# Retention and expert layers on one core: two more units fetched in pieces, and routing's constants two half units later

## The chip, the cores and the metric

The kernel runs on one core of a Trainium2 chip. The metric is the device time in microseconds (us) of one execution. The engines of the core work side by side, each through its own instructions in a fixed order: TensorE (PE; PEld is its weight load), VectorE (DVE), ScalarE (ACT), GpSimd (POOL) and SyncE (SP, which here only issues transfers). They wait for each other and for transfers through semaphores.

## The reference

Two layers follow each other.

```python
scores = scale * np.matmul(q, k.transpose(0, 1, 3, 2))      # 8 batches, 8 heads, 576 positions, 64 wide
gamma = 1.0 - 2.0 ** (-5.0 - np.arange(H))
Dmat = np.where(rel >= 0, gamma ** rel, 0.0)                # rel = query position - key position
x = np.matmul(scores * Dmat, v)                             # then 4608 tokens x 512
logits = x @ w_gate                                         # 8 experts, 576 tokens each at most
# all (token, expert) logits from the largest down: a token goes to the first expert that has room
out[mask] = np.maximum(x[mask] @ w1[e], 0.0) @ w2[e]        # 512 -> 1024 -> 512, expert by expert
```

## The kernel before

The first layer (`attention`, the first 125 us or so) is cut into 16 units, each two batches by two heads; a unit takes two half units, g = 0 and g = 1, so half unit 2u+g runs from 0 to 31. A unit needs four arrays: `q` and `k` (128 x 1152, transposed), `v` (128 x 1152) and `n` (128 x 1024, keys in rows). Decay is split into blocks of 128 positions: within a block a masked product, between blocks a running state.

What each engine does for unit u, in the order in which it does it:

- POOL: `qscale` multiplies `q` by decays in place, in three instructions (columns 0 to 512, 512 to 1024, 1024 to 1152; L619); then `kscale` makes `ks` from `n` in two instructions (L624). For units 2 and up all five are emitted together at the end of unit u-2 (L878 to L880), so POOL meets them in just this order: three of `q`, then two of `ks`.
- PE: `scores` (L634, L639), `update` (L655: state += ks' v; `pS`), `from_states` (L669) and `from_blocks` (L678, L684) into `px`. In half unit 2u+1 PE runs `scores` of unit u+1's first half, and then `update(u+1, 0)`, the first user of that unit's `ks` and `v`.
- DVE: `masks` (L644 `at`, L646 `am`) multiplies the scores by the decay mask. ACT copies the state out (`st`, L658) and the output (`xT`, L693).

Every engine takes its instructions in the order in which the code emits them; nothing is rearranged. Work that has its place between the units hangs in a table: `at(i, f)` puts f at the end of half unit i, and `fills` runs what stands there. Routing's preparation hangs there: `setup` (twelve steps of DVE memsets and ACT copies that read the constants `rc_f`), `share` (four DVE copies, L169 to L172, that put small constants into the PSUM tile `PT`, columns 288 to 475) and, from half unit 8 on, `logits` (PE, L710, writes columns from 0 of the same tile `PT`) and `logits2` (DVE reads them).

Transfers: units 0 and 1 come in pieces (columns up to 512, then the rest), the others whole. SP issues them from one queue. Each transfer has one of eight semaphores in turn, and SP waits before it issues one until the transfer that last had that semaphore has landed: eight are under way at most. `ahead(u)` and the loop around it (L816, L851, L863) issue what comes next; the tiles of four units (three of `n`) fit.

After the first layer come a search that fills the experts in turn and, per expert, a gather, two matrix products (L1110, L1153) and a scatter. Weights are fetched once the search has named the expert. Nothing there is touched.

Of the kernel before, what the change touches and what calls it, by code (L numbers as in the profile page):

```python
# [558 lines left out]
def attention(tc, nc, P, qk, vk, cst_d, wg_d, rf, xd, Lg, raw):  # L559
# [17 lines left out]
    def load(u, what, cuts=None):  # L577

        bp, hp = divmod(u, HP)
        for i in what:  # L580
            n = 1024 if i == "n" else 1152
            t = P['ld'].tile([128, n], F32, name=i + "in", bufs=3 if i == "n" else 4)
            src = qk[bp, hp, "qk".index(i)] if i in "qk" else vk[bp, hp, :, :1152] if i == "v" else vk[bp, hp, :, 1152:]
            LD[u, i] = t
            if cuts:
                pieces[u, i] = [(t[:, a:b], src[:, a:b]) for a, b in zip((0,) + cuts, cuts + (n,))]
            else:
                nc.sync.dma_start(t, src)

    pieces = {}  # L590
# [14 lines left out]
    R = Route(P['c'], P['a'], P['ps'], Lg, P['ident'])  # L605
# [4 lines left out]
    PT = P['ps'].tile([128, 512], F32, name="pT", tag="t")  # L610
# [166 lines left out]
    def at(g, f, *a):  # L777
        fill.setdefault(g, []).append((f, a))
# [8 lines left out]
        at(2*hp - 2, decays, hp)  # L787
    setup = R.setup()
    for i in range(12):
        at(4 + i, lambda: next(setup, None))  # L790
    at(6, lambda: R.share(PT[:, 288:475]))
    for bp in range(NP - 1):
        for i, x in enumerate(((0, 4), (4, 9))):
            at(8*(bp+1)+2*i, logits, bp, *x)
# [20 lines left out]

    def ahead(u):  # L816
        if u == 0:
            load(2, "qknv")
            load(3, "qkn")
            R.fetch(nc, rf)  # L820
        if u + 3 < 16:
            load(u + 3, "v")
        if u == 1:
            for b in range(2):
                for h in range(2):
                    nc.sync.dma_start(wg[64*h:64*h+64, :, b, 0:8], wg_d.rearrange("(hp h p) e -> h p hp e", h=2, p=64)[h ^ b])
# [18 lines left out]
    last = 15  # L845
    for u in range(16):
        ahead(u)
        for g in range(2):
            n, m = (u, u + 1)[g], (1, 0)[g]
# [375 lines left out]
def build(tc, nc, qk, vk, cst, wg, rf, w1, w1n, w2, out):  # L1225
    with ExitStack() as top:
# [23 lines left out]
        with ExitStack() as ctx:  # L1250
            P['wt'] = "px"
            P['pp'] = ctx.enter_context(tc.tile_pool(name="a_ps", bufs=1, space=bass.MemoryType.PSUM))
            Q = dict(P)
            for name, bufs in (("a", 1), ("ld", 2), ("w", 2), ("xt", 2)):
                Q[name] = ctx.enter_context(tc.tile_pool(name="a_" + name, bufs=bufs))
            R, rows = attention(tc, nc, Q, qk, vk, cst, wg, rf, xd, Lg, P['raw'])

            def idle(what):

                if what in ("row", "rows"):  # L1260
                    for i in range(2):
                        if rows:
                            if i or what == "rows" or len(rows) < 14:
                                rows.pop(0)()
                        elif i or what == "rows":
                            warm(1 + (what == "rows"))
                    what = 0
                if what:
                    warm(what)
            R.idle = idle  # L1270
            run = moe(tc, nc, P, R, xd, (w1, w1n), w2, out, mix)
            mix.drain(lambda: 0 in run.regs)
            while rows:
                rows.pop(0)()
# [22 lines left out]
```

## Time and profile before

| | us |
|---|---|
| median of 3 runs | 610.39 (610.30 to 612.76) |
| profiled execution | 610.37 |
| its span (first to last instruction) | 608.6 |
| PE busy | 593.4 |
| POOL busy | 245.8 |

The profile is of one execution. Its span leaves 1.77 us around it. "PE busy 98%" counts overlapping matmuls as busy and is no measure of peak; what matters below is where PE has nothing to do, and for whom it then waits.

### The profile page before, as it was taken

The numbers are of one execution on the slowest core, as the hardware profiler recorded it, in microseconds if no ns is written. First come the engines' busy times: TensorE is split into PE (matmuls) and PEld (weight loads), VectorE is DVE, ScalarE is ACT, GpSimd is POOL, SyncE is SP. The second block draws the span as 40 slices with busy tenths as digits, with TensorE's granted clock in tenths as the row PEclk, the third lists the DMA queues.
The fourth block names the chain that finished last, engine by engine and source line by source line (L and its number), as shares of the span: only waits on it lengthen the run. The fifth ranks groups of instructions, "written<-read, shape, count | busy, mean of one in ns | idle before, by whom it ended". The sixth has DMA issues, their size and how long they took to land.

```text
span 608.6 us, 14908 instructions
## 1 busy us (share of the span) xinstructions
PE 593.4 (98%) x5778; PEld 515.2 (85%) x5778; DVE 421.6 (69%) x1510; ACT 254.3 (42%) x446; POOL 245.8 (40%) x313
## 2 busy tenths in 40 slices
PE   8899999999999999999999999999999999999994
PEld 5788888875798889879977997898899889989983
DVE  5647687787899878878866885788488845544400
ACT  2344333334563654434561554266244334423310
POOL 5778456613411641441431243133224758610021
PEclk9999999999999999999999999999999999999998
DMA  9999999766786798794985699288938734420010
GB/s 324 407 367 403 306 358 378 254 198 205 190 224 149 224 263 162 259 246 124 263 231 153 135 251 248 85 195 242 249 90 193 229 119 146 150 78 27 2 44 34
DMA packets 49450, 124.84 MB, mean 205 GB/s; under 512 B 7011, under 2 KB 19811, under 8 KB 49379
## 3 DMA queue, kind: packets, MB, share of 16 engines
q1 hardware_dynamic: 36130, 80.10, 37.5%
q0 software_dynamic: 13104, 43.53, 31.5%
q8 instruction: 45, 0.74, 0.5%
q10 hardware_dynamic: 144, 0.26, 0.1%
q14 instruction: 27, 0.21, 0.1%
HBM read 80.35 MB, written 18.87 MB: 163 GB/s over the span
## 4 chain that ended last, share of the span: by engine, by line
PE 77%; issue 12%; DMA 5%; POOL 3%; DVE 2%; SPq 0%; ACT 0%; POOLq 0%; DVEq 0%
PE ph L1110 29%; PE py L1153 26%; PE sc L634 5%; PE px L678 4%; PE pS L655 3%; DMA vin<-in_vk 3%; PE px L669 3%; PE pt L1074 2%; PE r L383 2%; PE pT L710 2%; POOL out_y L1130 1%; POOL xg L1030 1%; PE r L489 1%; DMA kin<-in_qk 1%; DMA raw<-in_w 1%
## 5 line engine op out<-in xcount | busy, mean ns | idle before, releaser
L1153 PE MATMUL py<-w2h,hb 128*128 128x512 f32 x576 | 187.3, 397 | 0.0
L1110 PE MATMUL ph<-xh,w1h 128*128 128x320 f32 (+1 forms) x512 | 151.9, 301 | 0.2 <-ACT xh L1076 0.2
L1110 PE MATMUL ph<-xl,w1h 128*128 128x320 f32 (+1 forms) x512 | 149.2, 296 | 0.0
L1110 PE MATMUL ph<-xh,w1l 128*128 128x320 f32 (+1 forms) x512 | 149.0, 296 | 0.0
L1153 PE MATMUL py<-w2l,hb 128*128 128x512 f32 (+1 forms) x320 | 125.1, 391 | 0.0
L1153 PEld LDWEIGHTS py<-w2h,hb 128*128 128x128 f32 x576 | 104.5, 188 | 21.7
L1110 PEld LDWEIGHTS ph<-xh,w1h 128*128 128x128 f32 x512 | 96.0, 189 | 1.3 <-ACT xh L1076 0.7
L1114 ACT ACTIVATE hb<-ph 128x256 fp32r<-128x256 f32 (+1 forms) x128 | 52.4, 409 | 106.0 <-PE ph L1110 104.2
L1110 PEld LDWEIGHTS ph<-xl,w1h 128*128 128x128 f32 x512 | 96.2, 190 | 0.3
L1110 PEld LDWEIGHTS ph<-xh,w1l 128*128 128x128 f32 x512 | 96.0, 189 | 0.0
L1130 POOL DMA_INDIRECT out_y<-yt,idx x40 | 40.2, 1004 | 129.3 <-ACT yt L1173 67.0
L1119 DVE SCALAR_TENSOR_TENSOR hb<-ph,hb 128x256 fp32r<-128x256 f32 (+1 forms) x192 | 57.8, 350 | 26.1 <-ACT hb L1114 25.4
L1153 PEld LDWEIGHTS py<-w2l,hb 128*128 128x128 f32 (+1 forms) x320 | 56.7, 177 | 13.0
L619 POOL TENSOR_TENSOR qin<-qin,cst 128x512 f32<-128x512 f32 (+1 forms) x48 | 47.7, 1020 | 35.5 <-DMA qin<-in_qk 31.5
L1173 ACT ACTIVATE yt<-py 128x512 f32<-128x512 f32 x31 | 18.5, 598 | 92.3 <-PE py L1153 66.3
L658 ACT ACTIVATE st<-pS,cst 128x128 f32<-128x128 f32 x64 | 23.6, 368 | 75.0 <-PE pS L655 75.0
L1009 POOL DMA_DIRECT2D w2l<-raw x24 | 21.7, 905 | 73.3 <-ACT w2l L1008 36.8
L646 DVE TENSOR_TENSOR am<-sc,cst 128x1024 f32<-128x1024 f32 x32 | 39.0, 1218 | 15.9 <-PE sc L634 15.9
L1042 POOL DMA_INDIRECT xg<-xd,idx x30 | 30.4, 1015 | 42.7 <-DVE room L524 16.1
L1030 POOL DMA_INDIRECT xg<-xd,quarter x36 | 36.9, 1026 | 10.8 <-issue 8.1
L1009 POOL DMA_DIRECT2D w1l<-raw x23 | 21.1, 933 | 41.9 <-ACT w1l L1008 33.6
L634 PE MATMUL sc<-qin,kin 64*128 64x128 f32 x512 | 37.5, 286 | 0.2 <-DMA kin<-in_qk 0.2
(213 smaller groups left out, 931.8 us busy)
## 6 DMA issues: line engine op xcount, KB each, us to landing
raw<-in_w SPq DMA_DIRECT2D x56, 512.0 KB, 5.8
w2l<-raw POOLq DMA_DIRECT2D x24, 512.0 KB, 6.8
w1l<-raw POOLq DMA_DIRECT2D x23, 512.0 KB, 6.9
qin<-in_qk SPq DMA_DIRECT2D x14, 576.0 KB, 7.6
kin<-in_qk SPq DMA_DIRECT2D x14, 576.0 KB, 8.8
vin<-in_vk SPq DMA_DIRECT2D x14, 576.0 KB, 9.9
nin<-in_vk SPq DMA_DIRECT2D x14, 512.0 KB, 8.6
xd<-raw SPq DMA_DIRECT2D x36, 128.0 KB, 5.2
```

Source lines behind the costliest of these rows:

```text
L619: nc.gpsimd.tensor_tensor(x, x, e[:, None, :n].to_broadcast([128, (b-a)//n, n]), op=ALU.mult)
L634: nc.tensor.matmul(t[:, h, 128*j:128*j+128], blk(k, 4*g+j)[r], blk(q, 4*g+j)[r], start=(j == 0), stop=True, skip_group_check=True)
L646: nc.vector.tensor_tensor(a, SC[u, g].rearrange("p h (j q) -> p h j q", q=128), m1[:, u % HP, :, None, :].to_broadcast([128, 2, 4, 128]), ...
L678: nc.tensor.matmul(PX[u, g][y:y+64, b, 128*c:128*c+128], blk(v, 4*g+j)[:, 64*h:64*h+64], AM[u, g][:, h, j], start=False, stop=True, skip_g ...
L1009: add = lambda: nc.gpsimd.dma_start(lo, raw, accum_op=ALU.add)
L1030: nc.gpsimd.indirect_dma_start(out=t[:, k, :], out_offset=None, in_=xq[:, :], in_offset=bass.IndirectOffsetOnAxis(ap=quarters[e][:, v:v+1] ...
L1042: nc.gpsimd.indirect_dma_start(out=xg[:n, j, :], out_offset=None, in_=xd[:, :], in_offset=bass.IndirectOffsetOnAxis(ap=found[e][:n, j:j+1] ...
L1110: T.matmul(ps, w, x, start=(k == 0), stop=(k == 11))
L1114: A.activation(hb[:, f, c], ps, AF.Relu)
L1119: V.scalar_tensor_tensor(hb[:, f, to+a:to+b], ps[:, a:b], 0.0, hb[:, f, 256*s+a:256*s+b].bitcast(F32), op0=ALU.max, op1=ALU.subtract)
L1130: st = nc.gpsimd.indirect_dma_start(out=out[:, :], out_offset=bass.IndirectOffsetOnAxis(ap=found[e][:n, t:t+1], axis=0), in_=y[:n], in_off ...
L1153: T.matmul(ps[:m], a, w, start=(k == 0), stop=(k == last), skip_group_check=True)
```

## The change

```diff
     setup = R.setup()
     for i in range(12):
-        at(4 + i, lambda: next(setup, None))
-    at(6, lambda: R.share(PT[:, 288:475]))
+        at(6 + i, lambda: next(setup, None))
+    at(8, lambda: R.share(PT[:, 288:475]))
...
     def ahead(u):
         if u == 0:
-            load(2, "qknv")
-            load(3, "qkn")
+            for x in (2, 3):
+                load(x, "kqnv", (512,))
+                for _ in range(2):
+                    for i in "kqnv":
+                        nc.sync.dma_start(*pieces[x, i].pop(0))
             R.fetch(nc, rf)
-        if u + 3 < 16:
+        elif u + 3 < 16:
             load(u + 3, "v")
```

Units 2 and 3 now come as units 0 and 1 do: the first 512 columns of k, q, n and v, then the rest of k, q, n and v. The constants `rc_f` (610 columns, 305 KB) follow all of unit 3, where they stood ahead of its `v`. All twelve steps of `setup`, and `share`, run two half units later.

On SP, whose rows are transfers, in the place after the second piece of unit 1's `v`: eight rows of before,

```order
L588 DMA qin<-in_qk 128x1152 [waits DMAHW2_49]
L588 DMA kin<-in_qk 128x1152 [waits DMAHW3_49]
L588 DMA nin<-in_vk 128x1024 [waits DMAHW4_49]
L588 DMA vin<-in_vk 128x1152 [waits DMAHW5_49]
L588 DMA qin<-in_qk 128x1152 [waits DMAHW6_49]
L588 DMA kin<-in_qk 128x1152 [waits DMAHW7_49]
L588 DMA nin<-in_vk 128x1024 [waits DMAHW0_49,Pool_49]
L101 DMA rc_f<-in_rf 128x610 [waits DMAHW1_49]
```

and the eight of the change, which are unit 2 alone:

```order
L822 DMA kin<-in_qk 128x512 [waits DMAHW2_49]
L822 DMA qin<-in_qk 128x512 [waits DMAHW3_49]
L822 DMA nin<-in_vk 128x512 [waits DMAHW4_49]
L822 DMA vin<-in_vk 128x512 [waits DMAHW5_49]
L822 DMA kin<-in_qk 128x640 [waits DMAHW6_49]
L822 DMA qin<-in_qk 128x640 [waits DMAHW7_49]
L822 DMA nin<-in_vk 128x512 [waits DMAHW0_49]
L822 DMA vin<-in_vk 128x640 [waits DMAHW1_49]
```

The whole `q` stood first; now its second piece is the sixth transfer of its unit.

On POOL, unit 2's five instructions (`qin` is `q`, `ks` the scaled keys; "waits DMAHW7" is a wait for a transfer), before:

```order
L619 TENSOR_TENSOR qin<-qin,cst 128x512 [waits DMAHW2_49]
L619 TENSOR_TENSOR qin<-qin,cst 128x512
L619 TENSOR_TENSOR qin<-qin,cst 128x128
L624 TENSOR_TENSOR ks<-nin,cst 128x512 [waits DMAHW4_49,PE_49,Pool_49]
L624 TENSOR_TENSOR ks<-nin,cst 128x512
```

and of the change:

```order
L619 TENSOR_TENSOR qin<-qin,cst 128x512 [waits DMAHW3_49]
L619 TENSOR_TENSOR qin<-qin,cst 128x512 [waits DMAHW7_49]
L619 TENSOR_TENSOR qin<-qin,cst 128x128
L624 TENSOR_TENSOR ks<-nin,cst 128x512 [waits DMAHW4_49,PE_49,Pool_49]
L624 TENSOR_TENSOR ks<-nin,cst 128x512 [waits DMAHW0_49]
```

The order is the same; the second instruction has a wait of its own, for the second piece of `q`, and both `ks` stand behind it.

On PE, at the end of half unit 8, where the first `logits` stand (`pT` is the tile `PT`), before:

```order
L655 MATMUL pS<-vin,ks 64x64 [waits Activation_49]
L655 MATMUL pS<-vin,ks 64x64 x3
L710 MATMUL pT<-xT,wg 32x128 [waits DMAHW7_49,DMAHW0_49]
L710 MATMUL pT<-xT,wg 32x128
L710 MATMUL pT<-xT,wg 32x128 [waits DMAHW2_49,DMAHW1_49]
L710 MATMUL pT<-xT,wg 32x128 x13
```

and of the change:

```order
L655 MATMUL pS<-vin,ks 64x64 [waits Activation_49]
L655 MATMUL pS<-vin,ks 64x64 x3
L710 MATMUL pT<-xT,wg 32x128 [waits DMAHW7_49,DMAHW0_49,DVE_49]
L710 MATMUL pT<-xT,wg 32x128
L710 MATMUL pT<-xT,wg 32x128 [waits DMAHW2_49,DMAHW1_49]
L710 MATMUL pT<-xT,wg 32x128 x13
```

The first of them waits for DVE now. On DVE `share`, which writes `pT` too, stands in half unit 8 directly behind that half unit's `am`:

```order
L644 TENSOR_TENSOR at<-px,cst 128x256 [waits PE_49]
L646 TENSOR_TENSOR am<-sc,cst 128x1024
L169 COPY pT<-rc_f 128x128
L170 COPY pT<-rc_f 128x8 [waits DVE_49]
L171 COPY pT<-sm 128x10 [waits DVE_49]
L172 COPY pT<-inc 128x5 [waits DVE_49]
```

In the program the semaphore count for which the first `logits` wait is that of the fourth of these copies, L172.

## Rows read from the trace of the kernel before

**Rows 1.** The page, chain that ended last: shares of the span by engine.

```profile
PE 77%; issue 12%; DMA 5%; POOL 3%; DVE 2%; SPq 0%; ACT 0%; POOLq 0%; DVEq 0%
```

**Rows 2.** Chain that ended last, in order of time: start us, us, what.

```profile
7.26 5.79 DMA vin<-in_vk
...
13.07 10.12 DMA vin<-in_vk
```

**Rows 3.** Timeline of PE: start us, us, instruction, count [idle before <-releaser].

```profile
19.46 0.94 PE L669 MATMUL px<-qin,st 64*64 64x128 f32 x24
20.63 1.16 PE L634 MATMUL sc<-qin,kin 64*128 64x128 f32 x16 [0.22 <-DMA kin<-in_qk]
23.32 0.45 PE L655 MATMUL pS<-vin,ks 128*64 128x64 f32 x8 [1.53 <-DMA vin<-in_vk]
...
30.19 0.45 PE L655 MATMUL pS<-vin,ks 128*64 128x64 f32 x8
```

**Rows 4.** Waits of PE from 23 to 125 us: total us, times, longest.

```profile
PE pS L655 <- DMA vin<-in_vk: 1.5, 1, 1.5
```

**Rows 5.** Timeline of SP's queue: issues of unit 1.

```profile
5.60 0.43 SPq L602 DMA_DIRECT2D kin<-in_qk  x1
...
10.38 0.33 SPq L602 DMA_DIRECT2D vin<-in_vk  x1
```

**Rows 6.** Transfers issued from 9.8 to 10.6 us: count, KB, us to landing.

```profile
vin<-in_vk SPq DMA_DIRECT2D x1, 320.0 KB, 7.3
```

**Rows 7.** Transfers issued from 5.5 to 6.4 us.

```profile
kin<-in_qk SPq DMA_DIRECT2D x1, 256.0 KB, 5.4
```

**Rows 8.** Timeline of POOL.

```profile
8.24 1.69 POOL L619 TENSOR_TENSOR qin<-qin,cst 128x512 f32<-128x512 f32 x2 [0.84 <-DMA qin<-in_qk]
9.88 1.04 POOL L624 TENSOR_TENSOR ks<-nin,cst 128x512 f32<-128x512 f32 x1
...
19.13 2.91 POOL L619 TENSOR_TENSOR qin<-qin,cst 128x512 f32<-128x512 f32 x3 [1.21 <-DMA qin<-in_qk]
22.00 2.04 POOL L624 TENSOR_TENSOR ks<-nin,cst 128x512 f32<-128x512 f32 x2
...
32.60 2.92 POOL L619 TENSOR_TENSOR qin<-qin,cst 128x512 f32<-128x512 f32 x3 [2.90 <-DMA qin<-in_qk]
35.48 2.04 POOL L624 TENSOR_TENSOR ks<-nin,cst 128x512 f32<-128x512 f32 x2
```

**Rows 9.** Busy time by stretch: engines (instructions), PEclk, DMA share, GB/s.

```profile
9.00:12.00 3.00, 3.00 (x58) 2.64 (x60) 1.23 (x3) 0.74 (x2) 2.33 (x5) 1.00 1.05 396
...
21.00:24.00 3.00, 1.47 (x31) 1.31 (x30) 3.00 (x4) 0.13 (x1) 3.00 (x4) 1.00 1.01 403
```

**Rows 10.** Timeline of DVE, half units 6 and 8.

```profile
34.06 1.21 DVE L646 TENSOR_TENSOR am<-sc,cst 128x1024 f32<-128x1024 f32 x1
35.20 0.28 DVE L169 COPY pT<-rc_f 128x128 f32<-128x128 f32 x1
...
35.92 0.17 DVE L172 COPY pT<-inc 128x5 int32<-128x5 int32 x1
...
40.94 1.21 DVE L646 TENSOR_TENSOR am<-sc,cst 128x1024 f32<-128x1024 f32 x1
```

**Rows 11.** Timeline of PE, half unit 8.

```profile
41.96 1.08 PE L710 MATMUL pT<-xT,wg 128*32 128x128 f32 x32
```

**Rows 12.** Line L1248 (warm-up matmuls) to 8 us: duration ns min/median/max, first, last.

```profile
L1248 PE MATMUL warm<-full x12: 607/634/634, 1.5 to 6.1; 128*128 128x512 bf16 x12
```

**Rows 13.** The same line from 100 to 200 us.

```profile
L1248 PE MATMUL warm<-full x49: 376/379/395, 142.1 to 157.9; 128*128 128x512 bf16 x49
```

**Rows 14.** Busy time by stretch, the end (columns as in rows 9).

```profile
600.00:605.00 5.00, 0.68 (x4) 0.22 (x2) 0.41 (x1) 0.40 (x1) 0.96 (x1) 0.96 0.14 52
605.00:608.60 3.60, 0.00 (x0) 0.00 (x0) 0.00 (x0) 0.00 (x0) 0.00 (x0) 0.50 0.00 0
```

**Rows 15.** Timeline of PE, its last matmul.

```profile
600.29 0.39 PE L1153 MATMUL py<-w2l,hb 128*128 128x512 f32 x1
```

## The prediction

> **What bounds the kernel now.** I read the chain of waits first. It runs over PE for most of the span and over DMA for 5% [rows 1]; put in order of time, its DMA part lies in the first 23 us, and its last piece there is unit 2's whole `v`, issued at 13.07 and landed 10.12 later, at 23.19 [rows 2]. From there on the reader should see only PE. The timeline of PE shows what that transfer holds: `scores` of unit 2 at 20.63 after 0.22 us of waiting for `k`, and `update(2, 0)` at 23.32 after 1.53 us of waiting for `v` [rows 3]. The view of PE's waits from 23 to 125 us has that one row alone [rows 4], so from 23.32 to the end of the first layer PE has no other wait worth naming, and everything after (search, weights, experts) hangs on PE's results. A microsecond gained or lost at `update(2, 0)`, or by a wait put into PE's row later, therefore moves the end by a microsecond. At most the two waits, 0.22 + 1.53 = 1.75 us, can be gained.
>
> But `update(2, 0)` has two parents. It also wants POOL's first `ks` of unit 2. In POOL's timeline [rows 8] the three `q` instructions start at 19.13 and the two `ks` at 22.00, 1.04 us each (a lone one, 9.88, shows it): the first is ready at 23.04. It is 0.15 us earlier than `v`. So taking `v` away uncovers POOL at once.
>
> **The pieces of unit 2.** When do they land? All transfers share one queue and land in turn. The last piece of unit 1 was issued at 10.38 [rows 5] and took 7.3 [rows 6]: it landed at 17.68. From there to 23.19 the four whole transfers of unit 2, 576 + 576 + 512 + 576 = 2240 KB, took 5.51 us, 2.46 us per 1000 KB. Pieces are a little slower: unit 1's first `k` piece landed at 5.60 + 5.4 = 11.00 [rows 5, 7], its first `v` piece, three pieces of 256 KB later, at 7.26 + 5.79 = 13.05 [rows 2]: 2.05 us for 768 KB, 2.67 per 1000 KB. These are the two bounds. In the change unit 2's pieces come as k, q, n, v of 256 KB, then k and q of 320 KB: the second piece of `q` ends 1664 KB after 17.68, at 17.68 + 4.09 = 21.77 by the one, at 17.68 + 4.44 = 22.12 by the other. I take the middle, 21.95.
>
> POOL now. The first piece of `q` (512 KB after 17.68, at about 19.0) finds POOL idle, as before (its 1.21 us of idling ended at 19.13). Its first instruction ends near 20.3, and PE, whose `from_states` ends at 19.46 + 0.94 = 20.40, goes into `scores` without a wait, to 20.40 + 1.16 = 21.56. There the 0.22 is gained. But then POOL stands before the second part of `q`, whose piece lands at 21.95, and the `ks` instructions stand behind it. What is left to do from that landing to the end of the first `ks` is what unit 0 shows in the same form: two `q` instructions at 8.24, and `ks` to 9.88 + 1.04 = 10.92, 2.68 us [rows 8]. With 0.08 us from landing to start and 0.1 us from POOL to PE (`v`'s hand-over took 23.19 to 23.32), `update(2, 0)` starts at 21.95 + 0.08 + 2.68 + 0.1 = 24.81 instead of 23.32: **+1.5 us** (1.3 to 1.7 between the two rates). `v`'s first piece has long landed (1000 KB after 17.68, near 20.3) and its wait is gone; what is late next is POOL.
>
> A wait in POOL's row is passed on to what is queued behind it. The second `ks` of unit 2 ends about 1 us later, near 25.7, and `update(2, 2)` comes over 3 us after `update(2, 0)`: covered. Unit 3: its second `q` piece lands one unit (2240 KB, 5.5 to 6.0 us) after unit 2's, at 27.5 to 28.1, its first `ks` is ready 2.8 us after that, at 30.3 to 30.9. Before, `update(3, 0)` ran at 30.19 [rows 3], so 1.5 us later it runs at 31.7 and finds it there. This cover is the first delay itself. Unit 4 is whole again; its `q` started on POOL at 32.60, and the bytes ahead of it are the same, so its `ks` (35.48 + 1.04 = 36.5) comes when it did, with PE 1.5 us later.
>
> **More transfers.** Units 2 and 3 come in 16 pieces instead of 8 whole transfers. An issue takes SP 0.33 to 0.43 us [rows 5], 8 more take some 3 us of SP's time over the 15 us in which they are issued, and SP idles between issues, since it waits for one of eight semaphores each time: no cost, as the queue stays full. The stretch from 9 to 12 us, all pieces, moved 396 GB/s, that from 21 to 24 us, whole transfers, 403 [rows 9]: the price of pieces, already in the upper bound above. The landings of pieces follow each other by 0.68 us [rows 2, 5, 7]. The Trainium skill (DMA: Bandwidth & Descriptors, Anatomy of one DMA) speaks against more and smaller transfers: about 2 us fixed for each. By that, as an estimate from the page, eight more, one after another, would cost 16 us and the sum would be near 629; the landings don't bear it out here, since transfers under way together share that time, and I give it no chance.
>
> **Constants two half units later.** `rc_f` lands behind unit 3's `v`, near 30, where its first user now stands in half unit 6 (DVE was at 34.06 there): covered. The ACT copies of `setup` sit in ACT's idle time in any half unit and nobody waits for them soon: nothing. Moving DVE's memsets costs nothing either; half unit 6 loses `share` and gains them.
>
> `share` is another matter. In half unit 6 nobody on PE touched `pT` for two half units. In half unit 8 PE's first `logits` write the same tile, and they now wait for the fourth copy (shown in the order of PE's rows above). In half unit 6 `share` ended at 35.92 + 0.17 = 36.09, 2.03 us after the `am` ahead of it began, at 34.06 [rows 10]. In half unit 8 `am` began at 40.94, so `share` would end at 40.94 + 2.03 = 42.97 on the old clock. PE came to the `logits` at 41.96 [rows 11]. With 0.06 us of hand-over PE stands for 42.97 + 0.06 - 41.96 = **1.07 us**. DVE's `am` hangs on PE's matmuls, so both have shifted alike and the difference holds. Bounds: 0, were DVE done earlier, and 1.3 if the copies run a third slower beside POOL. I take 1.07: they ran beside POOL in half unit 6 too (32.60 to 37.5).
>
> **Sum.** Against the profiled execution's own 610.37 (0.02 below the median of the runs): 610.37 + 1.5 + 1.07 = **612.9 us**, +0.42%. About 0.5%, 3.05 us, is what a measurement of this kernel can tell from no change, so the forecast is a small loss inside "same", its own range 612.2 to 613.5.
>
> **Rivals.**
>
> 1. The clock falls: the side of "slower". PE stands idle from 21.56 to 24.81, 3.25 us, in one piece. The trace has waits of 1.53 us at most in this layer, and the granted clock stays 1.00 there [rows 9]. It falls once: the last matmul ends at 600.68 [rows 15], and the stretch from 600 to 605 averages 0.96, the next is 0.50 [rows 14], the 1.2 GHz level; 0.04 lacking of 5 us at half speed is 0.4 us, so the fall came near 604.6, 3.9 us after the matmul. 3.25 us lies between the wait that did nothing and the one that did. Price: at the start of the kernel the warm-up matmuls take 634 ns each [rows 12], later 379 [rows 13], and all twelve, from 1.5 to 6.7 us, are slow, so half speed lasts 5.2 us or more after work begins and loses half of that, 2.6 us: 612.9 + 2.6 = 615.5. It decides once the idle piece comes near 3.9 us. The Trainium skill (TensorE: Matmul & The Clock Gate, HAM oscillation) describes such a fall between bursts that wait for transfers. No wait in this trace is long enough to tell. Chance 0.15.
>
> 2. POOL is not held: the second `q` piece lands so early that `ks` is back at 23.0 or before, which takes a landing by 20.2. The landings above give at least 21.77, against it [rows 2, 5 to 7]. Only `share` would cost: 610.4 + 1.07 - 0.1 = 611.4. Chance 0.1.
>
> 3. The change does what it says and `share` does not hold PE: both waits go, 610.37 - 1.75 = 608.6. It needs an early `ks` and a DVE that runs ahead; neither row gives it. Chance 0.04. With only `share` not in the way it is 611.9: chance 0.06.
>
> **Numbers.** Forecast 0.65, the rivals 0.15, 0.1, 0.04 and 0.06. The range 611.2 to 614.8 holds the forecast, rival 2, the second half of rival 3 and what of rival 1 ends with a short slow spell, some 0.84. Slower by over 0.5% (above 613.4): rival 1 and a tenth of the forecast's part, 0.23. Faster by over 0.5% (below 607.3) would need more than the two waits hold: 0.03. The rest, 0.74, is same.
>
> **What would show it.** Right: POOL's second `q` instruction of unit 2 idle until about 22 with the transfer as releaser; PE's `pS` of unit 2 idle about 3.2 us until POOL's `ks`, at 24.8; PE's first L710 idle about 1.1 us until DVE's L172, and PE without other new waits to 125 us. Wrong: `pS` of unit 2 before 23.5; no wait at L710; a granted clock under 1.00 after 24 us (rival 1); or a new wait of unit 3's `update` on POOL, which would add what it shows.

## The result and the profile after

| | before | change |
|---|---|---|
| median of six runs each, us | 611.13 (610.30 to 612.76) | 615.56 (614.56 to 616.02) |
| profiled execution, us | 610.37 | 615.68 |
| its span, us | 608.6 | 613.9 |
| mean granted clock of that execution | 0.997 | 0.994 |

The ratio is 1.0065, 95% interval 1.0047 to 1.0084: slower by 0.65%, 2.7 us above the forecast of 612.9 and 0.8 above the end of its range.

The two views that show it at once are PE's waits from 23 us to the last `logits` (total us, times, longest), which answer to [rows 4]:

```profile
PE pS L655 <- POOL ks L624: 3.1, 1, 3.1
PE px L669 <- issue: 1.1, 1, 1.1
PE pT L710 <- DVE pT L172: 1.0, 1, 1.0
```

and PE's timeline around unit 2, which answers to [rows 3] (start us, us, instruction, count, idle before and its releaser):

```profile
20.50 1.16 PE L634 MATMUL sc<-qin,kin 64*128 64x128 f32 x16
24.81 0.45 PE L655 MATMUL pS<-vin,ks 128*64 128x64 f32 x8 [3.15 <-POOL ks L624]
25.09 1.15 PE L678 MATMUL px<-am,vin 128*64 128x128 f32 x16
...
27.66 1.93 PE L634 MATMUL sc<-qin,kin 64*128 64x128 f32 x16
...
33.20 0.45 PE L655 MATMUL pS<-vin,ks 128*64 128x64 f32 x8
```

The wait for `v` and the 0.22 us before `scores` are gone. In their place stands one wait of 3.15 us for POOL's `ks`, and `update(2, 0)` starts at 24.81 instead of 23.32. But a second thing is in these rows: `scores` of the next half unit takes 1.93 us where the same sixteen matmuls take 1.16 above, and `update(3, 0)` comes 8.39 us after `update(2, 0)`, where it took 30.19 - 23.32 = 6.87 [rows 3]. The windows (columns as in [rows 9]) name the reason:

```profile
21.00:24.00 3.00, 0.66 (x12) 0.47 (x10) 1.24 (x2) 0.00 (x0) 1.92 (x3) 1.00 1.05 386
24.00:27.00 3.00, 2.19 (x40) 2.10 (x40) 0.00 (x0) 0.37 (x1) 2.98 (x3) 0.82 1.05 386
27.00:30.00 3.00, 3.00 (x38) 2.53 (x38) 0.14 (x1) 0.96 (x2) 2.02 (x3) 0.61 1.01 395
30.00:33.00 3.00, 3.00 (x72) 2.69 (x66) 2.34 (x6) 1.22 (x3) 1.67 (x2) 1.00 1.02 401
```

The third column from the right is the granted clock: 1.00 until 24, then 0.82 and 0.61, then 1.00 again. It fell about 1 us after the idle piece had ended; from 26 to 29 us it is 0.50, the lower level of 1.2 GHz. Over the six microseconds 0.18 x 3 + 0.39 x 3 = 1.71 us of full speed are lacking.

POOL's timeline, which answers to [rows 8], shows where the 3.15 us come from:

```profile
19.06 1.28 POOL L619 TENSOR_TENSOR qin<-qin,cst 128x512 f32<-128x512 f32 x1 [0.97 <-DMA qin<-in_qk]
22.08 1.68 POOL L619 TENSOR_TENSOR qin<-qin,cst 128x512 f32<-128x512 f32 x2 [1.74 <-DMA qin<-in_qk]
23.72 2.04 POOL L624 TENSOR_TENSOR ks<-nin,cst 128x512 f32<-128x512 f32 x2
```

POOL stands 1.74 us before the second piece of `q`, and `ks`, for which PE waits, is behind it. Later, DVE's `share` (to be set against [rows 10]) and PE's first `logits` (against [rows 11]):

```profile
43.94 1.21 DVE L646 TENSOR_TENSOR am<-sc,cst 128x1024 f32<-128x1024 f32 x1
45.07 0.28 DVE L169 COPY pT<-rc_f 128x128 f32<-128x128 f32 x1
...
45.80 0.17 DVE L172 COPY pT<-inc 128x5 int32<-128x5 int32 x1
```

```profile
46.02 1.18 PE L710 MATMUL pT<-xT,wg 128*32 128x128 f32 x32 [0.98 <-DVE pT L172]
```

The fourth copy ends at 45.97 and the `logits` start at 46.02. The last wait, near the end of the layer, is of another kind:

```profile
106.82 0.77 PE L669 MATMUL px<-qin,st 64*64 64x128 f32 x22
108.69 0.27 PE L669 MATMUL px<-qin,st 64*64 64x64 f32 x2 [1.10 <-issue]
```

PE stops inside a row of 24 matmuls, between the 22nd and the 23rd, and nothing that the profile shows releases it. So the start of PE's landmarks, after against before:

| | before | change | later by |
|---|---|---|---|
| `update(2, 0)` | 23.32 | 24.81 | 1.49 |
| `update(3, 0)` | 30.19 | 33.20 | 3.01 |
| first `logits` | 41.96 | 46.02 | 4.06 |
| `logits` of the last unit | 126.17 | 131.82 | 5.65 |
| last matmul | 600.29 | 605.58 | 5.29 |

The steps: 1.49 POOL, 1.52 clock, 1.05 `share`, 1.59 from there to the last `logits` (1.10 of it the stop at issue), -0.36 behind the first layer. They sum to 5.29, the span grew by 5.3. (These are two executions; how far `update(2, 0)` moves between executions stands below.)

### The profile page after: what moved, and what is told of

Its sections match the earlier page's. It is cut to its first block, busy times and chain, and to the rows that moved or that the text cites. A ratio compares the mean times of both kernels' runs of the same rounds, so it can differ in the third digit from the quotient of the medians.

```text
span 613.9 us, 14919 instructions
## 1 busy us (share of the span) xinstructions
PE 594.3 (97%) x5776; PEld 516.3 (84%) x5778; DVE 417.6 (68%) x1510; ACT 253.2 (41%) x446; POOL 246.9 (40%) x313
## 4 chain that ended last, share of the span: by engine, by line
PE 76%; issue 12%; DMA 4%; DVE 3%; POOL 3%; SPq 1%; ACT 0%; another core or an unknown queue 0%; POOLq 0%; DVEq 0%
PE ph L1113 28%; PE py L1156 25%; PE sc L634 5%; PE px L678 4%; DMA qin<-in_qk 3%; PE pS L655 2%; PE px L669 2%; PE r L383 2%; PE pt L1077 2%; PE pT L710 2%; POOL out_y L1133 1%; PE r L489 1%; DMA xg<-xd,idx 1%; PE r L327 1%; PE px L684 1%
## 5 line engine op out<-in xcount | busy, mean ns | idle before, releaser
L1033 POOL DMA_INDIRECT xg<-xd,quarter x36 | 38.2, 1060 | 11.5 <-issue 9.4
```

Source lines behind the costliest of these rows:

```text
L1033: nc.gpsimd.indirect_dma_start(out=t[:, k, :], out_offset=None, in_=xq[:, :], in_offset=bass.IndirectOffsetOnAxis(ap=quarters[e][:, v:v+1] ...
```

## The experiments

The theory after the result: four causes, of which the second hangs on the first. (a) POOL's order: `ks` behind the second `q` piece. (b) The granted clock falls because PE idles for long; it is a consequence of (a). (c) `share` in the half unit of the first `logits`. (d) The stop at issue. The rivals: that 16 pieces, not the idling, are at fault for (b); that (a) is only a matter of where the wait shows, because unit 4's arrival sets the pace; and for (d), that it belongs to the change, or that it moves with anything.

Each version was timed in rounds with the kernel before. "Low" counts the runs whose mean granted clock was 0.994 or less, as it was in the execution above (0.0028 of 614 us is the 1.71 us). It is a sign of a fall and doesn't show its place. The fourteen profiled executions bear it out: the three with a fall in the first layer have means of 0.993 and 0.994, the eleven without 0.995 to 0.997. The last two columns are of one profiled execution each. Diffs are against the change, e8's against the kernel before.

| version | median us | ratio to before, 95% | low | update(2,0) to (3,0) | first to last `logits` |
|---|---|---|---|---|---|
| before | 610.83 to 611.15 | | 6 of 105 | 6.87 | 84.21 |
| change | 615.56 | 1.0065 [1.0047, 1.0084] | 5 of 6 | 8.39 | 85.80 |
| e1 late constants alone | 612.52 | 1.0018 [1.0003, 1.0032] | 2 of 12 | 6.87 | 86.01 |
| e2 pieces alone | 614.41 | 1.0047 [1.0032, 1.0062] | 6 of 12 | 6.87 | 86.62 |
| e3 13 matmuls in the gap | 613.32 | 1.0043 [1.0028, 1.0059] | 1 of 12 | 6.87 | 84.60 |
| e4 POOL's order | 612.23 | 1.0020 [1.0004, 1.0036] | 0 of 12 | 6.87 | 87.39 |
| e5 the same, `share` early | 611.64 | 1.0016 [0.9995, 1.0038] | 2 of 12 | 6.86 | 84.77 |
| e6 5 matmuls in the gap | 613.72 | 1.0061 [1.0035, 1.0087] | 2 of 7 | 6.86 | 85.73 |
| e7 code moved | 614.49 | 1.0060 [1.0037, 1.0082] | 5 of 8 | 8.38 | 84.63 |
| e8 before, POOL late | 614.01 | 1.0054 [1.0033, 1.0075] | 7 of 10 | 8.38 | 84.57 |
| e9 order for all units | 612.89 | 1.0034 [1.0007, 1.0062] | 1 of 12 | 6.87 | 88.08 |
| e10 before, code moved by 13 | 610.74 | 0.9994 [0.9979, 1.0009] | 0 of 12 | 6.87 | 83.96 |
| e11 before, code moved by 64 | 613.73 | 1.0043 [1.0029, 1.0058] | 1 of 12 | 7.65 | 86.12 |
| e12 e5 with code moved | 611.77 | 1.0011 [0.9997, 1.0026] | 0 of 12 | 6.87 | 85.34 |

**e1_late_only: the constants two half units later, the transfers as before.**

```diff
-            for x in (2, 3):
-                load(x, "kqnv", (512,))
-                ...
-        elif u + 3 < 16:
+            load(2, "qknv")
+            load(3, "qkn")
+        if u + 3 < 16:
```

> The transfers as before, only the setup steps and share two half units later. Theory (the loss has three places: POOL's second part of q 1.5 us, the clock's fall after the idle piece 1.5 us, share in front of the first logits 1.05 us): update(2,0) stays at 23.3, the granted clock at 1.00, PE idles about 1.0 us before the first L710 until DVE's L172; the time is 1.0 us above the kernel before. Rival (the later constants cost nothing, DVE runs ahead): no wait at L710 and the time of the kernel before. Second rival (all of the loss beyond the POOL term comes from the constants): 3 us above.

PE waits 0.98 us at the first `logits` for L172, as in the change, and for `v` of unit 2 as before. So (c) is worth 1.0 us by itself. In this profile two waits of 0.62 and 0.70 us, up to 75.74 and 106.54, are put down to POOL's `qin`. The first is another: POOL's instruction had ended at about 75.2, and PE went on at a row of the kind that is found under e11 below, 2.2 us after a packet of code. The second also stands at such a row, but POOL ended just then too; the two causes can't be told apart there.

**e2_pieces_only: the pieces, constants and `share` in their old half units.**

```diff
-        at(6 + i, lambda: next(setup, None))
-    at(8, lambda: R.share(PT[:, 288:475]))
+        at(4 + i, lambda: next(setup, None))
+    at(6, lambda: R.share(PT[:, 288:475]))
```

> The pieces and the place of the constants' transfer as in the change, the setup steps and share in the half units of before. Theory: update(2,0) at 24.8 with 3.1 us of idling until POOL's ks, the granted clock near 0.8 and 0.6 in the stretches 24 to 27 and 27 to 30 us, no wait at the first L710; 3.0 us above the kernel before, 1.0 us below the change. Rival (share costs nothing of its own since PE would be late anyway): the time of the change, 4 to 4.5 us above before.

The wait at `logits` is gone, (a) stays: 3.02 us of waiting for `ks`, `update(2, 0)` at 24.53. The profiled execution shows no fall of the clock:

```profile
24.00:27.00 3.00, 2.47 (x54) 2.23 (x56) 0.00 (x0) 0.94 (x3) 2.72 (x3) 1.00 1.05 394
```

but 6 of its 12 runs had the low clock, with a median of 615.08 against 613.94 of the other six. The fall is thus no fixed part of the change: after 3.0 us of idling it did not come in this execution, and the low runs suggest that it comes in others. The two ratios, 1.0018 and 1.0047, each known to some 0.0015, together give the change's 1.0065.

**e3_fill13: the change, with 13 matmuls that nobody reads, in the gap.**

```diff
+                if (n, m) == (2, 0):
+                    for _ in range(13):
+                        nc.tensor.matmul(PT, P['full'][:, :128], P['full'], start=True, stop=True)
```

> The change with 13 matmuls of 128x512 bf16 on PE between scores of unit 2's first half and update(2,0), 2.8 us of PE work that nobody reads, in the idle piece. Theory (the idle piece lets the clock fall): update(2,0) still starts at 24.8, the granted clock stays 1.00, update(3,0) comes 6.9 us after update(2,0) instead of 8.4; 1.5 us below the change. Rival (the slow stretch from 25 to 29 us belongs to the pieces' traffic or to POOL, not to the idling): granted clock and distance as in the change, and its time. Second rival (the matmuls delay update(2,0)): it starts later than 24.9, and the gain is smaller by as much.

```profile
21.46 2.98 PE L860 MATMUL pT<-full 128*128 128x512 bf16 x13
24.44 0.45 PE L655 MATMUL pS<-vin,ks 128*64 128x64 f32 x8
...
31.31 0.45 PE L655 MATMUL pS<-vin,ks 128*64 128x64 f32 x8
```

`update(2, 0)` is as late as in the change, but `update(3, 0)` follows after 6.87 us, the clock is 1.00 and 1 run of 12 has the low one. The median is 2.24 us below the change's. Not all of it is the clock's (1.52 in the profiles): the stop near 108 us is gone as well, which 13 matmuls more in PE's row can do by themselves (e7 below has as many, and no filling: its stop is gone, its clock fell). The pieces are all there: (b) needs the idling. One profile would not show that, since e2's has no fall either; the counts do. Where PE idled for 2.7 us or more in one piece (the change, e2, e7, e8), 23 of 36 runs are low; in the five versions that have the pieces and no idle piece at `update(2, 0)` (e3, e4, e5, e9, e12), 4 of 60.

**e6_fill5: the same with 5 matmuls.** The diff is that of e3 with `range(5)`.

> The change with 5 instead of 13 filling matmuls: 1.1 us of PE work at the start of the idle piece, 2.0 us of idling left. Theory (the length of the idle piece decides): the clock stays, the mean clock over the runs is 0.996 as before and with 13, the time as with 13 (2.4 us above the kernel before). Rival (any idling of this kind lets it fall): mean clock 0.993 to 0.994 and 4 us above before.

1.76 us of idling were left, no fall in the profile, 2 low runs of 7; its interval of seven runs doesn't tell it from the change.

**e8_before_idle: the kernel before, no pieces, with POOL kept busy ahead of unit 2's first `ks`.**

```diff
+            for _ in range(2 * (u == 2)):
+                nc.gpsimd.memset(KS[u], 0.0)
```

> The kernel before, whole transfers and all, with two memsets of unit 2's ks on POOL ahead of its first ks, 1.2 us each: update(2,0) at 25.5, PE idle 3.7 us in one piece. Theory (idling alone lets the clock fall): granted clock 0.5 for some 3 us after 25.5, update(3,0) 8.4 us after update(2,0); mean clock over the runs 0.993 to 0.994; 2.2 + 1.5 = 3.7 us above the kernel before. Rival (the pieces' transfers are part of it): clock 0.996, 2.2 us above.

The two memsets took 1.98 us together, less than I had reckoned with, and still:

```profile
25.00 0.69 PE L657 MATMUL pS<-vin,ks 128*64 128x64 f32 x8 [3.35 <-POOL ks L626]
...
33.38 0.45 PE L657 MATMUL pS<-vin,ks 128*64 128x64 f32 x8
```

```profile
24.00:27.00 3.00, 2.00 (x24) 2.00 (x26) 0.19 (x1) 0.37 (x1) 3.00 (x3) 0.66 1.03 403
27.00:30.00 3.00, 3.00 (x50) 2.59 (x48) 0.00 (x0) 0.96 (x2) 3.00 (x5) 0.78 1.03 414
```

Whole transfers, the old constants, and the fall is there, with 0.34 x 3 + 0.22 x 3 = 1.68 us lacking and 8.38 us between the two updates. That refutes the rival for (b) from the other side: a wait for POOL is enough, without the pieces.

**e4_pool_order: the change, with POOL's order for units 2 and 3 as the pieces land.**

```diff
+                if u < 2:
+                    qscale(u + 2, (0, 512))
+                    kscale(u + 2, 0, 8)
+                    qscale(u + 2, (512, 1024), (1024, 1152))
+                else:
                     qscale(u + 2, (0, 512), (512, 1024), (1024, 1152))
                     kscale(u + 2, 0, 8)
```

> The change with POOL's instructions of units 2 and 3 in the order of the pieces: first part of q, first ks, the other two parts of q, second ks. Theory (POOL waits for the second q piece with ks behind it): first ks of unit 2 ends near 21.4, update(2,0) starts near 21.6 right behind scores, no idle piece, clock 1.00, and 1.75 us are gained on before there; share still holds the first L710 for 1.0 us; 0.7 us below the kernel before, 4.8 to 5.2 us below the change. Rival (n's or v's first piece lands late too): update(2,0) near 23.3 and 1 us above before. Second rival (the wait moves to scores of unit 2's second half, which needs the second pieces): half of the gain is given back within 3 us.

In POOL's row the first `ks` now stands ahead of the second `q` piece, which leaves PE without a wait at 21.46, 1.86 us earlier than before:

```profile
18.51 1.27 POOL L619 TENSOR_TENSOR qin<-qin,cst 128x512 f32<-128x512 f32 x1 [0.72 <-DMA qin<-in_qk]
19.75 1.04 POOL L624 TENSOR_TENSOR ks<-nin,cst 128x512 f32<-128x512 f32 x1
21.52 1.69 POOL L619 TENSOR_TENSOR qin<-qin,cst 128x512 f32<-128x512 f32 x2 [0.74 <-DMA qin<-in_qk]
...
32.60 2.93 POOL L619 TENSOR_TENSOR qin<-qin,cst 128x512 f32<-128x512 f32 x3 [2.48 <-DMA qin<-in_qk]
35.48 2.06 POOL L624 TENSOR_TENSOR ks<-nin,cst 128x512 f32<-128x512 f32 x2
```

With that (a) is gone, and no run of twelve has the low clock, but the gain doesn't reach the end, and the expected 0.7 us below the kernel before was missed: PE then waits 0.68 us for unit 4's `ks`, 0.98 for `share`, and 0.21, 0.76 and 1.30 at issue. This profiled execution took 614.07 us, 1.84 above the median of its runs, so these stops are not all typical.

**e5_pool_order_share6: e4, with `setup` at `5 + i` and `share` at 6.** The diff is e4's and these two numbers.

> As the last kernel (POOL's instructions of units 2 and 3 in the order of the pieces), and share back in half unit 6, the setup steps from half unit 5 on. Theory A (the gain at update(2,0) lives on): update(2,0) at 21.5, no wait at the first L710, 1.9 us below the kernel before, 3.3 us below the last kernel. Theory B (a PE that is early runs into transfers that are not, into POOL waiting for q and into waits that end at issue): only share's 1.0 us is gained on the last kernel, the time is that of the kernel before within 0.6 us, and the profile has waits of together 1.5 to 2 us for POOL or for issue between 30 and 118 us.

```profile
21.36 0.45 PE L655 MATMUL pS<-vin,ks 128*64 128x64 f32 x8
...
36.79 0.45 PE L655 MATMUL pS<-vin,ks 128*64 128x64 f32 x8 [1.47 <-POOL ks L624]
```

1.96 us gained at unit 2, 1.47 of it waited for at unit 4, whose `q` lands when it did (POOL begins it at 32.82, before at 32.60 [rows 8]). First `logits` at 41.69, before 41.96. It is level with the kernel before, no better. The kernel before shows why, in PE's timeline:

```profile
37.06 0.45 PE L655 MATMUL pS<-vin,ks 128*64 128x64 f32 x8
```

This is `update(4, 0)`, and unit 4's first `ks` is ready at 35.48 + 1.04 = 36.52 [rows 8]. So of the two waits that the change set out to remove, only about 0.5 us could be gained; the rest would have been waited for one whole unit later.

**e9_both: POOL's order for every unit, constants behind unit 4's `v`, `setup` at `7 + i`, `share` at 9.**

```diff
-                qscale(u + 2, (0, 512), (512, 1024), (1024, 1152))
+                qscale(u + 2, (0, 512))
                 kscale(u + 2, 0, 8)
+                qscale(u + 2, (512, 1024), (1024, 1152))
```

> Units 2 and 3 in pieces; on POOL, in every unit from 2 on, the first part of q, the first ks, the rest of q, the second ks; the constants fetched behind unit 4's v; setup steps from half unit 7 on and share in half unit 9, behind the first logits. Theory (the early PE of the last such kernel lost 1.5 us at update(4,0) to POOL's ks of unit 4, which stood behind three q instructions and a later transfer): update(2,0) at 21.4, the wait at update(4,0) under 0.3 us, no wait of the first L710 for DVE, first L710 at 40.1 instead of 42.0; median 1.5 to 1.9 us below the kernel before. Rival (whatever PE gains early is taken by later transfers): update(5,0) or a later unit waits as much, and the time is that of the kernel before within 0.6 us.

It was missed. No wait at unit 4, none at the first `logits`, which start at 41.01, 0.95 us before those of the kernel before. Then 88.08 us to the last ones instead of 84.21, of which 1.25 and 0.53 us are stops at issue (105.06 and 112.32). Of the other 2 us some 1.3 are five smaller gaps between PE's instructions, 0.17 to 0.35 us each, at rows of the kind that is found under e11 below; the rest isn't placed.

**e7_code_shift: the change, its twelve warming matmuls of 512 columns cut into 25 of 246.** The work is the same; 13 matmuls more, with a weight load each, move all that follows in PE's code.

```diff
-    P['warm'](12)
+    P['warm'](25, 246)
...
-        def warm(n):
+        def warm(n, m=512):
...
-                nc.tensor.matmul(ps, full[:, :128], full, start=True, stop=True)
+                nc.tensor.matmul(ps[:, :m], full[:, :128], full[:, :m], start=True, stop=True)
```

> The change with the 12 warm-up matmuls of 512 columns at the program's start replaced by 25 of 246: the same work, 26 instructions more, as many as the 13 filling matmuls add, so that every later PE instruction stands 26 places further on. Theory (the idle piece let the clock fall, and the 1.1 us at 108.7 us, whose wait ends at issue, is PE waiting for its own instructions at a place that repeats by instruction count): update(2,0) at 24.8 with 3.1 us of idling, mean clock 0.993 to 0.994 as in the change; waits that end at issue, if there are any, stand 26 instructions earlier than the last two matmuls of L669 in half unit 24. Time 3 to 4.5 us above before. Rival (the 13 filling matmuls gained by moving the instructions, not by the clock): the time of that kernel, 2.4 us above before.

The stop near 108 us is gone and the median is 1.07 us lower, though the intervals overlap. In this profile the clock fell after 2.73 us of idling (0.51 from 24 to 27, 0.92 to 30: 1.71 us lacking again): less idling than in e2, where it had not.

**e10_before_shift13, e11_before_shift64, e12_level_shift13: the same cut in the kernel before (25 of 246, and 76 of 81), and in e5 (25 of 246).**

> The kernel before, with the twelve warming matmuls cut into 25 of 246 columns: same columns, 13 matmuls more in PE's row, nothing else moved. Code theory (the waits that end at issue, near 105 to 109 us, come from where PE's code is cut into the 16 KB pieces in which it is fetched): the pieces end elsewhere in the row, so this kernel, without pieces of units and without a late share, can show such a wait of 0.5 to 1.3 us, or a span from the first to the last row of logits other than 84.2 us by 0.5 or more. Transfer theory (they come from the order of the data's transfers, which is the same as before here): no such wait, 84.2 +- 0.3 us, and 610.4 to 611.5 in all.

> The kernel before, with the twelve warming matmuls cut into 76 of 81 columns: 64 matmuls more in PE's row. Code theory: the ends of the pieces of code stand at yet another place, and the span from first to last logits differs from that of the kernel with 13 more, and perhaps from the 84.2 us of before, by 0.5 to 2 us. Transfer theory: 84.2 +- 0.3 us here too, no wait that ends at issue.

> The level version (POOL's order changed, setup one half unit later, share in half unit 6) with 13 matmuls more by the same cut. Code theory: the 84.8 us from first to last logits move by 0.3 or more either way, and the median moves with them from 611.6. Transfer theory: 84.8 +- 0.3 and 611.6 +- 0.5. Neither expects it to beat the kernel before by over 0.5%.

e10 shows no stop and the time of the kernel before, so moving the code need not cost anything. e11, in which no transfer, no constant and no order is changed, is 0.43% slower. PE's timeline of e11:

```profile
27.74 0.94 PE L669 MATMUL px<-qin,st 64*64 64x128 f32 x23
29.16 0.21 PE L669 MATMUL px<-qin,st 64*64 64x64 f32 x1 [0.49 <-issue]
...
47.50 0.37 PE L634 MATMUL sc<-qin,kin 64*128 64x128 f32 x1
48.78 1.05 PE L634 MATMUL sc<-qin,kin 64*128 64x128 f32 x14 [0.91 <-issue]
```

Two stops inside rows of matmuls, 1.40 us together, at places where the kernel before has none. Here the transfer theory fails: the place of the code alone brings such stops. What PE stops for can be read in the transfers. Of the change, 106.25 to 106.45 us (queue: packets, MB, share):

```profile
q1 hardware_dynamic: 20, 0.08, 97.0%
q8 instruction: 1, 0.02, 30.5%
```

One packet of the instruction queue, 16 KB, between the data's at 97%; the stop ends at 108.69, 2.4 us after the packet began. The profiles up to 135 us have fifteen waits of 0.16 us or more at issue: one each in the change and e2, three each in e4, e6 and e9, two each in e11 and e12. Fourteen of them end 2.3 to 2.6 us after the start of such a packet; the exception is one of 0.16 us in e6.

The trace settles what these packets are. Number PE's instruction records in order of time (weight loads, matmuls, semaphore instructions). After the same fourteen stops PE goes on with records 962, 1730, 1986, 2754, 4034 or 4290 (one less in e6, where one matmul's record is missing). They all differ by multiples of 256, in seven kernels, though other work stands there in each (behind record 961 in e4 a matmul of L669, in e12 one of L684). One 16 KB packet begins for every 256 records, and from 15 to 115 us PE passed such a record in none of the fourteen profiles sooner than 2.2 us after the start of the latest packet. Around 100 us the packets of before are at 95.3, 100.3 and 106.5, those of the change at 92.7, 98.8 and 106.3: the one that PE stood for came 7.6 us behind the one ahead of it. So (d) is PE waiting for its own code: a packet that comes in time costs nothing, one that comes late costs the wait. In e12 a new stop of 0.74 us, up to 30.58, ends in the wait for unit 4's `ks`, which is 0.60 us instead of e5's 1.47, so it costs nothing there; from the first `logits` on 84.77 us became 85.34, as the code theory allows, while the median moved by 0.13, inside its interval: it decides nothing by itself.

## Why the prediction was wrong

- **What bounds the kernel: right for a loss, wrong for a gain.** A microsecond lost at `update(2, 0)` or in PE's row later was about a microsecond at the end: 5.65 us by the last `logits`, 5.29 at the last matmul. A gain is not passed on: of the two waits, put at 1.75 us, all but 0.5 would have been waited for at unit 4 (e5: 1.47 of 1.96 us). Since the time rose, this did not decide the miss; it does void rival 3's 608.6.
- **POOL, +1.5: right.** The second `q` piece was put at 21.95 and POOL began it at 22.08; `update(2, 0)` was forecast at 24.81 and began at 24.81. The mechanism is right; the last digits are luck: in the five profiles with these pieces and this order of POOL (the change, e2, e3, e6, e7) it began from 24.17 to 24.81, and in the four with whole transfers and nothing added on POOL (before, e1, e10, e11) from 22.84 to 23.71. e4 removes the wait by POOL's order alone.
- **The pieces as such, nothing: right.** They moved 386 to 401 GB/s in the stretches above, about the 396 of [rows 9], and landed when the sum said.
- **Unit 3 covered: right.** `update(3, 0)` waits for nobody. Unit 4's `ks` comes about when it did (first one ready at 36.5 before, 37.0 in the change), ahead of the late PE.
- **`share`, +1.07: right**, 0.98 of waiting and 1.05 at the landmark; e1 has it alone. The copies took 0.28 and 0.17 us, as in half unit 6 [rows 10]; the upper bound, copies a third slower beside POOL, had no row behind it.
- **The sum: the step that failed.** It carried the clock at 1.00 over the idle piece, and left the fall to rival 1 with a chance of 0.15. That rival's mechanism took place. The step in its wording that failed is "it decides once the idle piece comes near 3.9 us": that was read from the one fall in the trace, at the end of the kernel [rows 14, 15], and it is no bound. The clock fell after 2.73 us (e7), 3.15 (the change) and 3.35 (e8) in the profiles and not after 1.76 (e6), 2.05 (e10) and 3.02 (e2). Runs with 2.7 us or more of idling in one piece were low in 23 of 36. To carry the clock at 1.00 over 3.25 us of idling, between the 1.53 that did nothing and the 3.9 that did, was the wrong step.
- **Rival 1's price, 2.6, was too high.** It was taken from the warming matmuls at the start [rows 12]; the fall in the middle costs 8.39 - 6.87 = 1.52 us. With it the sum is 610.37 + 1.49 + 1.52 + 1.05 = 614.4, inside the range, which ended at 614.8: it took the next term too to leave it.
- **What no term held: 1.2 us.** 1.10 us of stop at issue, which is PE waiting for its code, and some 0.5 in smaller steps up to the last `logits` (among them two gaps of 0.2 us at rows of the same kind), less 0.36 regained behind. That the sum would be 615.5 with rival 1's price is chance: it was 1.1 too high and the stop 1.1 unforeseen.
- **Still open:** why in the change, whose diff alters none of PE's matmuls, the packet near 106 us came late. The transfers beside it, moved in time by 4 us, are likely, since the queues are full there, but no run takes them away. What decides, after about 3 us of idling, whether the clock falls in an execution is open too.

## What to carry to other kernels

Cutting a transfer in pieces moves the waits to the engine that works on the pieces: look at what stands behind the new wait in that engine's row, and put the instruction that feeds the bound engine ahead of it (e4: 3.15 us of waiting gone). Before counting a wait as its own length, ask what TensorE's clock does after it: a wait that is made longer, from 1.5 to 3.2 us, can cost half as much again in the matmuls behind it, and matmuls that nobody reads, put into the gap, held the clock here. Before counting a wait as a gain, see how much slack the next unit has behind it (0.5 us here). And where differences of 0.5% matter, time the kernel also with its code moved by some instructions: that alone cost 0.43% in e11 and nothing in e10.

## What the runs showed of the hardware

- Each fall of the clock in the first layer lacks about the same, 1.71, 1.71 and 1.68 us of full speed in the change, e7 and e8, and delays the work by 1.51 to 1.52 us. The Trainium skill (TensorE: Matmul & The Clock Gate, HAM oscillation) describes such falls between bursts that wait; these three profiles agree, and e2's, without a fall after 3.02 us, shows that the length of the idle piece alone doesn't settle it: e7's was shorter, 2.73 us.
- PE can stop inside a row of independent matmuls with no releaser in the profile, for 0.2 to 1.3 us. Fourteen of fifteen such stops end at instructions of PE's row that lie a multiple of 256 apart, 2.3 to 2.6 us after the start of a 16 KB packet of the instruction queue, in stretches where the data's transfers kept the DMA engines busy. A profile can put such a stop down to another engine (e1, 75.74).
